# Where the rounded gate and value blocks are stored from: SyncE's queue or ScalarE's

## The chip, the cores and the metric

The kernel runs on one core of a Trainium2 chip. The metric is the device time of one execution in microseconds. Three runs of the kernel before took 806.23, 806.28 and 807.58 us; the median is 806.28 us. The core's engines are named as in the profile: PE (matrix products; PEld is its weight load), DVE (VectorE), ACT (ScalarE), POOL (GpSimd) and SP (SyncE, which here only issues DMAs). ACT can issue DMAs as well, between its own instructions.

## The reference

Attention with a learned position bias is followed by a gated feed-forward layer. The weights of the second part arrive as float64.

```
scores = (q @ k.T) / 8 + bias(w1, b1, w2)            # 4 batches, 8 heads, 576 positions, 64 dims
attn   = softmax(scores) @ v                          # laid out as x: 2304 tokens x 512
gate   = 1 / (1 + exp(-(x @ w_gate)))                 # w_gate: 512 x 1536
val    = x @ w_val                                    # w_val:  512 x 1536
out    = (gate * val) @ w_out                         # w_out:  1536 x 512
```

## The kernel before

The program has three stages: the bias tables, the attention, and the feed-forward layer (class `Moe`), of which the first weights are prepared while the attention still runs. The layer cuts the 2304 tokens into six chunks of 384 (`T`), and the 1536 hidden columns into twelve blocks f = 0 to 11. For each f there are three weight blocks (f, z): z = 0 gate, z = 1 value, z = 2 output. Products are formed from a high and a low part of each factor, three matmuls for one.

The first two chunks go by plain products. `run` walks a fixed list `ORDER` of 24 units (chunk, f). In a unit PE forms `pg` and `pu` (`gates`, L888; one PSUM buffer each), then the products `po` of the unit before (`outs`, L912). ACT takes the sigmoid of `pg` (L897), DVE multiplies it with `pu` (L898), ACT copies the high part `gh` (L899) and DVE subtracts for the low part `gl` (L900). The next unit's `pg` can only begin when the sigmoid has read the last one. The other four chunks are done later by products of sums of weight blocks, which read the rounded blocks back from a buffer in HBM, `scratch` (L964).

Between the matmuls the weight blocks are prepared, one call of `convert` at a time, in the program's own order (`manual_schedule`: each engine runs its instructions in the order of the code). A block arrives by `stage` (L829, 512 KB, float64 as pairs of int32). `begin` gives it a buffer `wm` (a pool of five) and these steps, of which each call of `convert` does those that are due:

- step 0: ACT takes the size of the upper word (L198), the first write to `wm`
- step 1: DVE clamps it (L201); step 2: DVE rounds in three instructions (L204, L207, L210)
- step 3, `upper`: ACT copies the high part (L849)
- step 4, `lower`: DVE subtracts for the low part (L854), and `keep` stores the rounded block: gate and value blocks of f = 3 to 11, 18 in all, go to `scratch` (L860, 256 KB); output blocks go with both parts to `parts` (L858)

The blocks of f < 3 (`pre`) were rounded and stored in the bias stage and take no part in this. A sixth block needs a `wm` buffer that an earlier block has left, by its last reader and by its store.

Two rules of the framework matter for what waits. First, each DMA that SP or ACT issues is given one of eight completion semaphores, `DMAHW0` to `DMAHW7`, in turn in the order of the code, whichever engine issues it; before it is issued, its engine waits until the last DMA on that semaphore has landed. In the lists below `[waits DMAHW7_49]` at a DMA is this wait. Second, `wm` buffers are handed out when the program is built, and the instruction that first writes one waits for the last users of it.

Of the kernel before, what the change touches and what calls it, by code (L numbers as in the profile page):

```python
# [186 lines left out]
def narrow(nc, t, lo, hi, eng, sized=None):  # L187

    f = t.bitcast(F32)

    def size():
        if sized:
            sized.tensor_scalar(out=t, in0=hi, scalar1=0x7FFFFFFF, scalar2=None, op0=ALU.bitwise_and)
        else:
            nc.scalar.activation(out=f, in_=hi.bitcast(F32), func=AF.Abs)  # L198

    def clamp():  # L200
        eng.tensor_scalar(out=f, in0=f, scalar1=float(2.0 ** -15), scalar2=float(122880 - 2.0 ** -7), op0=ALU.max, op1=ALU.min)  # L201

    def low():
        nc.vector.tensor_scalar(out=t, in0=t, scalar1=3, scalar2=0x3FFFFFFF, op0=ALU.logical_shift_left, op1=ALU.bitwise_and)  # L204

    def top():
        nc.vector.scalar_tensor_tensor(out=t, in0=hi, scalar=-0x40000000, in1=t, op0=ALU.bitwise_and, op1=ALU.bitwise_or)  # L207

    def tail():
        nc.vector.scalar_tensor_tensor(out=t, in0=lo, scalar=29, in1=t, op0=ALU.logical_shift_right, op1=ALU.bitwise_or)  # L210

    return size, clamp, low, top, tail
# [498 lines left out]
class Moe:  # L711
# [121 lines left out]
    def begin(self):  # L833

        nc, n = self.nc, self.begun
        self.begun += 1
        f, z = b = self.blocks[n]
        w = self.raw.pop(0)
        if b in self.pre:
            m, steps = w, []  # L840
        else:
            t = self.pools["wm"].tile([128, 4, 128], I32, name="wm")
            m, steps = t.bitcast(F32), list(zip((0, 1, 2, 2, 2), narrow(nc, t, w[:, :, :, 0], w[:, :, :, 1], CLENG(nc, f, z))))

        def upper():
            p = self.pools["wfirst" if n < 3 or (z == 2 and n > 5) else "wa"]
            t = p.tile([128, 2, 4, 128], F32R, tag="w", name=f"w{z}_{f}")
            self.wts[b] = t[:, 0], t[:, 1], t
            nc.scalar.activation(out=t[:, 0], in_=m, func=AF.Copy)  # L849

        def lower():
            hi, lo, _ = self.wts[b]
            self.full.add(b)
            LOENG(nc, f, z).tensor_tensor(out=lo, in0=m, in1=hi.bitcast(F32), op=ALU.subtract)  # L854

        def keep():
            if z == 2:
                nc.sync.dma_start(out=self.parts[f], in_=self.wts[b][2].bitcast(F32))  # L858
            elif b not in self.pre:
                nc.sync.dma_start(out=self.scratch[b], in_=m)  # L860

        self.going[n] = steps + [(3, upper), (4, lower), (4 if z < 2 else 12 if f < 2 else 6, keep)]

    def convert(self):

# [321 lines left out]
```

## Time and profile before

| | |
|---|---|
| median of three runs | 806.28 us |
| profiled execution | 806.44 us, of which the span of instructions is 804.7 us |
| PE busy | 774.0 us, 96% of the span |
| DVE, ACT, POOL busy | 664.5, 490.5 and 341.8 us |
| plain products of the feed-forward layer | from about 367 to 502 us of the span |

The page of the profile gives busy time by engine. In the tables by stretch each engine has its busy time and, in brackets, its number of instructions; then come PE's granted clock as a share of full speed, the mean share of the DMA engines and GB/s. In the rows in order of time the first number is the start in us from the span's start, the second the duration, then engine, line and tiles; brackets give how long the engine had stood idle before, and what ended that. `SPq` and `ACTq` are DMAs as the engine issues them: the row shows the issue alone, not the transfer. In the list of waits: total us, times, longest us.

### The profile page before, as it was taken

The numbers are of one execution on the slowest core, as the hardware profiler recorded it, in microseconds if no ns is written. First come the engines' busy times: TensorE is split into PE (matmuls) and PEld (weight loads), VectorE is DVE, ScalarE is ACT, GpSimd is POOL, SyncE is SP. The second block draws the span as 40 slices with busy tenths as digits, with TensorE's granted clock in tenths as the row PEclk, the third lists the DMA queues.
The fourth block names the chain that finished last, engine by engine and source line by source line (L and its number), as shares of the span: only waits on it lengthen the run. The fifth ranks groups of instructions, "written<-read, shape, count | busy, mean of one in ns | idle before, by whom it ended". The sixth has DMA issues, their size and how long they took to land.

```text
span 804.7 us, 17534 instructions
## 1 busy us (share of the span) xinstructions
PE 774.0 (96%) x6356; PEld 722.6 (90%) x6356; DVE 664.5 (83%) x1397; ACT 490.5 (61%) x1046; POOL 341.8 (42%) x400
## 2 busy tenths in 40 slices
PE   7999989999999999889999999999999999999997
PEld 4888879999999998889889999898899999999996
DVE  6788888999999998996799898979878977776663
ACT  6888769989989987873444434543444435433432
POOL 1332659899999988950000000315232330423100
PEclk9999999999999999999999999999999999999999
DMA  5534435655655667739999643646334305421202
GB/s 197 172 126 144 121 88 149 172 146 155 174 152 152 177 183 206 205 113 277 354 303 276 174 145 131 202 138 218 107 112 140 105 27 193 148 62 70 79 1 79
DMA packets 66694, 124.22 MB, mean 154 GB/s; under 512 B 7344, under 2 KB 28976, under 8 KB 66608
## 3 DMA queue, kind: packets, MB, share of 16 engines
q1 hardware_dynamic: 64688, 120.15, 49.3%
q10 hardware_dynamic: 1920, 2.95, 1.2%
q8 instruction: 50, 0.82, 0.4%
q14 instruction: 36, 0.29, 0.1%
HBM read 86.04 MB, written 27.60 MB: 141 GB/s over the span
## 4 chain that ended last, share of the span: by engine, by line
PE 73%; DVE 14%; ACT 5%; issue 3%; DMA 3%; POOL 0%; SPq 0%; ACTq 0%; DVEq 0%
PE po L912 16%; PE pu L1010 10%; PE pg L1010 10%; PE sc L560 8%; PE acc L645 8%; PE pt L583 6%; PE pg L888 5%; PE pu L888 5%; PE bps L353 3%; DVE btmp L361 2%; ACT ind L334 2%; PE y L329 2%; PE pt L603 1%; DVE en L564 1%; DVE bias L369 1%
## 5 line engine op out<-in xcount | busy, mean ns | idle before, releaser
L971 POOL TENSOR_TENSOR ws<-wm 128x256 f32<-128x256 f32 x44 | 38.5, 875 | 309.5 <-DVE g L898 148.2
L567 ACT ACTIVATE en<-en,mn 128x576 f32<-128x576 f32 x144 | 111.6, 775 | 31.0 <-DVE mn L564 29.9
L560 PE MATMUL sc<-k,QS 128*128 128x288 f32 x640 | 112.1, 301 | 1.4 <-DVE bias L369 0.6
L1010 PE MATMUL pu<-xq,wv 128*128 128x384 f32 x504 | 102.7, 339 | 1.7 <-DVE g L898 0.6
L1010 PE MATMUL pg<-xq,wv 128*128 128x384 f32 x504 | 102.8, 339 | 0.4 <-DVE u L1015 0.4
L564 DVE CUSTOM_DVE_ANT_0 en<-sc,bias 128x576 f32<-128x576 f32 x128 | 93.8, 752 | 7.1 <-PE sc L560 6.1
L1010 PEld LDWEIGHTS pg<-xq,wv 128*128 128x128 f32 x504 | 90.2, 188 | 8.5 <-DVE u L1015 1.7
L1010 PEld LDWEIGHTS pu<-xq,wv 128*128 128x128 f32 x504 | 89.8, 188 | 8.5 <-DVE c L1015 1.2
L560 PEld LDWEIGHTS sc<-k,QS 128*128 128x128 f32 x640 | 92.3, 189 | 2.5 <-PE sc L560 0.8
L583 PE MATMUL pt<-ident,en 128*128 128x128 f32 x576 | 87.5, 274 | 3.5 <-DVE aL L483 1.9
L912 PE MATMUL po<-wo,gh 128*128 128x512 f32 x288 | 89.6, 392 | 0.0
L645 PE MATMUL acc<-aH,vv 128*128 128x288 f32 x240 | 76.2, 334 | 2.7 <-DVE xe L648 2.7
L583 PEld LDWEIGHTS pt<-ident,en 128*128 128x128 f32 x576 | 68.9, 141 | 6.7 <-ACT en L567 2.9
L483 DVE TENSOR_TENSOR aL<-pt,aH 128x512 fp32r<-128x512 f32 (+1 forms) x112 | 66.6, 607 | 7.1 <-ACT aH L482 7.1
L353 PE MATMUL bps<-cfs,ind 128*128 128x64 bf16 x1458 | 67.4, 193 | 2.9 <-DVE bias L369 2.4
L334 ACT ACTIVATE ind<-y 128x576 bf16<-128x576 f32 x100 | 62.1, 654 | 10.2 <-PE y L329 7.9
L645 PE MATMUL acc<-aL,vv 128*128 128x288 f32 x240 | 67.1, 296 | 0.0
L353 PEld LDWEIGHTS <-ind 128*128 128x128 bf16 x1458 | 58.6, 98 | 9.2 <-DVE bias L369 4.2
L487 POOL TENSOR_TENSOR aL<-ar,aH 128x512 fp32r<-128x512 f32 x48 | 62.4, 1301 | 4.0
L482 ACT ACTIVATE aH<-pt 128x512 fp32r<-128x512 f32 (+1 forms) x112 | 57.4, 527 | 1.1 <-PE pt L583 1.1
L912 PE MATMUL po<-wo,gl 128*128 128x512 f32 x144 | 56.7, 394 | 0.0
L888 PE MATMUL pg<-xhi,w 128*128 128x384 f32 x192 | 53.4, 337 | 1.8 <-ACT g L897 1.8
(158 smaller groups left out, 1860.0 us busy)
## 6 DMA issues: line engine op xcount, KB each, us to landing
wm<-scratch SPq DMA_DIRECT2D x48, 256.0 KB, 2.7
wo<-parts SPq DMA_DIRECT2D x24, 512.0 KB, 5.1
kr<-in_k_dram SPq DMA_DIRECT2D x32, 288.0 KB
QS<-part SPq DMA_DIRECT2D x64, 144.0 KB, 2.7
xs<-xe SPq DMA_DIRECT2D x32, 288.0 KB, 3.4
xin<-xs SPq DMA_DIRECT2D x48, 192.0 KB, 4.4
parts<-w SPq DMA_DIRECT2D x12, 512.0 KB, 2.7
vr<-in_v_dram SPq DMA_DIRECT2D x16, 320.0 KB, 3.9
```

The costliest lines, as they stand in the source:

```text
L334: nc.scalar.activation(out=o, in_=y[:, :, 0:HF], func=AF.Sigmoid, scale=float(2.0 ** 64))
L353: nc.tensor.matmul(out=o, lhsT=st, rhs=cfs[:, part], start=(part == 0), stop=(part == 2))
L483: return lambda: nc.vector.tensor_tensor(out=lo, in0=ps, in1=hi.bitcast(F32), op=ALU.subtract)
L487: nc.gpsimd.tensor_tensor(out=lo, in0=src, in1=hi.bitcast(F32), op=ALU.subtract)
L560: nc.tensor.matmul(out=ps[:, e, 0:HF], lhsT=l, rhs=r[:, HF * e:HF * e + HF], start=(i == 0), stop=(i == len(mms) - 1))
L564: nc.vector.tensor_tensor_reduce(out=half(en), in0=ps[:, :, 0:HF], in1=half(nbias), scale=-0.125, scalar=3.0e38, op0=ALU.add, op1=ALU.min, ...
L567: nc.scalar.activation(out=en, in_=en, func=AF.Exp, bias=mn, scale=-1.0, accum_out=sm)
L583: nc.tensor.transpose(pt[:, J], en[:, 128 * J:128 * J + 128], ident)
L645: nc.tensor.matmul(out=acc[:, 0:HF], lhsT=l, rhs=r, start=(i == 0), stop=(i == len(mms) - 1))
L888: self.nc.tensor.matmul(out=(pg, pu)[z], lhsT=l, rhs=r, start=(kc == 0 and i == 0), stop=(kc == 3 and i == 2))
L912: self.nc.tensor.matmul(out=po, lhsT=l[:, tt], rhs=r, start=(first and i == 0), stop=(last and i == 2))
L1010: nc.tensor.matmul(out=p, lhsT=W[i][:, l, at + kc], rhs=V[b][:, r, kc], start=(n == 0), stop=(n == 5))
```

## The change

The store `keep` of the 18 gate and value blocks is issued by ACT instead of SP, and stands directly behind `upper`, in the call of `convert` before that of `lower`. Output blocks and the blocks of f < 3 keep their steps.

```
             elif b not in self.pre:
-                nc.sync.dma_start(out=self.scratch[b], in_=m)
-
-        self.going[n] = steps + [(3, upper), (4, lower), (4 if z < 2 else 12 if f < 2 else 6, keep)]
+                nc.scalar.dma_start(out=self.scratch[b], in_=m)
+
+        self.going[n] = steps + [(3, upper), *([(3, keep), (4, lower)] if z < 2 and b not in self.pre else [(4, lower), (4 if z < 2 else 12 if f < 2 else 6, keep)])]
```

PE, DVE and POOL have the same instructions in the same order. On ACT, from the first such block on (block (3,0), `w0_3`; the numbers behind names count tiles), before:

```order
L849 ACTIVATE w0_3_7626<-wm_7561 128x512 [waits DVE_49]
L198 ACTIVATE wm_7625<-ww_7452 128x512 [waits DMAHW5_49]
L897 ACTIVATE g_7677<-pg_7642 128x384 [waits PE_49,Activation_49]
L899 ACTIVATE gh_7678<-g_7677 128x384 [waits DVE_49]
L849 ACTIVATE w1_3_7686<-wm_7605 128x512
L198 ACTIVATE wm_7683<-ww_7497 128x512 [waits DMAHW0_49]
L849 ACTIVATE w2_3_7698<-wm_7617 128x512 [waits DVE_49]
L198 ACTIVATE wm_7695<-ww_7512 128x512 [waits DMAHW4_49,DMAHW1_49,Activation_49]
```

and now:

```order
L849 ACTIVATE w0_3_7626<-wm_7561 128x512 [waits DVE_49]
L860 DMA scratch_59<-wm_7561 128x512 [waits DMAHW7_49]
L198 ACTIVATE wm_7625<-ww_7452 128x512 [waits DMAHW5_49]
L897 ACTIVATE g_7678<-pg_7643 128x384 [waits PE_49,Activation_49]
L899 ACTIVATE gh_7679<-g_7678 128x384 [waits DVE_49]
L849 ACTIVATE w1_3_7686<-wm_7605 128x512
L860 DMA scratch_59<-wm_7605 128x512 [waits DMAHW0_49]
L198 ACTIVATE wm_7684<-ww_7497 128x512
L849 ACTIVATE w2_3_7698<-wm_7617 128x512 [waits DVE_49]
L198 ACTIVATE wm_7696<-ww_7512 128x512 [waits DMAHW1_49,DVE_49]
```

The store stands between the copy of the high part and the next block's size, ahead of the sigmoid, and waits on semaphore 7. The size of block (4,2), the last row of each list, had the buffer of block (3,0) and waited for its store (semaphore 4); now it has the buffer of block (3,2) and waits for DVE, for the low part of that block.

On SP, from the load of value block (6,1) on, before:

```order
L829 DMA ww_7633<-in_moe_w_val_dram 128x4x256 [waits DMAHW7_49]
L798 DMA xin_7636<-xs_57 64x2x384 [waits DMAHW0_49]
L798 DMA xin_7636<-xs_57 64x2x384 [waits DMAHW1_49]
L807 DMA xrec_7639<-rs_58 64x384 [waits DMAHW2_49]
L807 DMA xrec_7639<-rs_58 64x384 [waits DMAHW3_49]
L860 DMA scratch_59<-wm_7561 128x512 [waits DMAHW4_49,DVE_49]
L829 DMA ww_7693<-in_moe_w_out_dram 128x1024 [waits DMAHW5_49]
L860 DMA scratch_59<-wm_7605 128x512 [waits DMAHW6_49,DVE_49]
L829 DMA ww_7705<-in_moe_w_gate_dram 128x4x256 [waits DMAHW7_49]
```

and now:

```order
L829 DMA ww_7634<-in_moe_w_val_dram 128x4x256 [waits DMAHW7_49]
L798 DMA xin_7637<-xs_57 64x2x384 [waits DMAHW0_49]
L798 DMA xin_7637<-xs_57 64x2x384 [waits DMAHW1_49]
L807 DMA xrec_7640<-rs_58 64x384 [waits DMAHW2_49]
L807 DMA xrec_7640<-rs_58 64x384 [waits DMAHW3_49]
L829 DMA ww_7694<-in_moe_w_out_dram 128x1024 [waits DMAHW4_49]
L829 DMA ww_7705<-in_moe_w_gate_dram 128x4x256 [waits DMAHW5_49]
L829 DMA ww_7753<-in_moe_w_val_dram 128x4x256 [waits DMAHW6_49]
L858 DMA parts_60<-w2_3_7698 128x1024 [waits DMAHW1_49,DVE_49]
```

The two stores have left the list, and three loads close up. Semaphore 7, which the load of value block (6,1) holds in both, was next used by a load of SP (gate block (7,0)); now its next user is the store of block (3,0) on ACT.

## Rows read from the trace of the kernel before

**Rows 1.** The page, busy time by engine.

```profile
PE 774.0 (96%) x6356; PEld 722.6 (90%) x6356; DVE 664.5 (83%) x1397; ACT 490.5 (61%) x1046; POOL 341.8 (42%) x400
```

**Rows 2.** By stretch: busy us by engine (instructions), granted clock, DMA share, GB/s.

```profile
382.00:392.00 10.00, 10.00 (x56) 9.59 (x55) 6.00 (x12) 3.92 (x7) 0.00 (x0) 1.00 1.06 389
392.00:402.00 10.00, 8.45 (x42) 7.09 (x40) 9.00 (x17) 4.34 (x8) 0.00 (x0) 1.00 1.08 319
402.00:412.00 10.00, 8.19 (x43) 7.46 (x44) 9.62 (x19) 5.41 (x11) 0.00 (x0) 1.00 1.07 311
412.00:500.00 88.00, 88.00 (x469) 82.82 (x468) 78.75 (x153) 37.23 (x73) 0.00 (x0) 1.00 0.65 201
```

**Rows 3.** Chain that ended last, 385 to 412: start, us, what.

```profile
394.02 6.99 DMA scratch<-wm
```

**Rows 4.** ACT in order of time, 388 to 402.

```profile
388.20 0.64 ACT L849 ACTIVATE w<-wm 128x512 fp32r<-128x512 f32 x1 [0.69 <-DVE wm L210]
...
389.95 0.49 ACT L897 ACTIVATE g<-pg 128x384 f32<-128x384 f32 x1 [0.57 <-PE pg L888]
...
399.21 0.69 ACT L198 ACTIVATE wm<-ww 128x512 f32<-128x512 f32 x1 [3.56 <-DMA scratch<-wm]
...
401.11 0.66 ACT L198 ACTIVATE wm<-ww 128x512 f32<-128x512 f32 x1 [0.69 <-DMA scratch<-wm]
401.68 0.47 ACT L897 ACTIVATE g<-pg 128x384 f32<-128x384 f32 x1
```

**Rows 5.** DVE in order of time, 392 to 409.

```profile
392.04 0.56 DVE L898 TENSOR_TENSOR g<-pu,g 128x384 f32<-128x384 f32 x1 [0.82 <-PE pu L888]
...
398.43 0.68 DVE L854 TENSOR_TENSOR w<-wm,w 128x512 fp32r<-128x512 f32 x1
...
402.18 0.56 DVE L898 TENSOR_TENSOR g<-pu,g 128x384 f32<-128x384 f32 x1 [0.94 <-ACT g L897]
...
408.10 0.55 DVE L900 TENSOR_TENSOR gl<-g,gh 128x384 fp32r<-128x384 f32 x1
```

**Rows 6.** PE in order of time, 393 to 409.

```profile
393.83 0.34 PE L888 MATMUL pg<-xhi,w 128*128 128x384 f32 x1
...
402.20 0.44 PE L888 MATMUL pg<-xhi,w 128*128 128x384 f32 x1 [1.76 <-ACT g L897]
...
408.71 0.50 PE L912 MATMUL po<-w,gl 128*128 128x512 f32 x1 [1.61 <-DVE gl L900]
```

**Rows 7.** SP's DMA issues in order of time, 386 to 397.

```profile
386.11 0.68 SPq L829 DMA_DIRECT2D ww<-in_moe_w_val_dram  x1
...
390.63 0.34 SPq L860 DMA_DIRECT2D scratch<-wm  x1
...
396.56 0.38 SPq L829 DMA_DIRECT2D ww<-in_moe_w_gate_dram  x1
```

**Rows 8.** What SP's queue waited for, 394.3 to 396.6: total, times, longest.

```profile
SPq L829 <- DMA ww<-in_moe_w_val_dram: 2.2, 1, 2.2
```

**Rows 9.** ACT and its own DMA issues, 364 to 373.

```profile
364.26 0.63 ACT L849 ACTIVATE w<-ww 128x512 fp32r<-128x512 f32 x1 [1.67 <-DMA ww<-scratch]
364.29 0.33 ACTq L826 DMA_DIRECT2D ww<-scratch  x1
...
371.71 0.38 ACTq L829 DMA_DIRECT2D ww<-in_moe_w_out_dram  x1
372.14 0.63 ACT L849 ACTIVATE w<-ww 128x512 fp32r<-128x512 f32 x1 [1.11 <-DMA xs<-xe]
```

**Rows 10.** SP's issue of the reciprocals in a later cycle.

```profile
426.90 1.19 SPq L807 DMA_DIRECT2D xrec<-rs  x2
```

**Rows 11.** ACT in that cycle, the copy ahead of store (7,1).

```profile
436.48 0.64 ACT L849 ACTIVATE w<-wm 128x512 fp32r<-128x512 f32 x1 [0.77 <-DVE wm L210]
```

**Rows 12.** By stretch, in the attention, columns as in rows 2.

```profile
312.00:315.40 3.40, 1.73 (x11) 1.35 (x12) 3.37 (x6) 2.30 (x6) 3.32 (x4) 1.00 0.48 152
315.40:318.80 3.40, 3.40 (x16) 3.40 (x17) 2.67 (x7) 2.08 (x5) 3.32 (x4) 0.50 0.58 170
```

## The prediction

> **What bounds the kernel now.** I read the page first: PE is busy for 774.0 of 804.7 us [rows 1], so nearly every microsecond that another engine loses costs nothing unless PE stands still for it, and what has to be found is where PE stands still near these stores. The table by stretch answers that. PE is busy without a gap from 382 to 392 and from 412 to 500, but it loses 1.55 us in 392 to 402 and 1.81 us in 402 to 412 [rows 2]. That is the start of the 18 stores; in the long stretch with most of them PE never waits. In the two stretches with losses DVE is busy for 9.00 and 9.62 of 10 us: beside PE it is the second engine that is nearly full there.
>
> The chain of waits puts 6.99 us of just this place on the transfer of a store [rows 3]. ACT in order of time shows where it bites: the size of a new block stands 3.56 us and then 0.69 us until a store has left its buffer [rows 4]. Behind them in ACT's order is the sigmoid at 401.68, for which PE waited 1.76 us, and DVE 0.94 us [rows 4 to 6]. PE's second loss, 1.61 us at 408.71, is for `gl`, which comes so late because DVE has a queue of work in front of it: from 402.18 to 408.10 it has no gap [rows 5, 6].
>
> So the most that an earlier store can bring is small. DVE works without a gap from 392.04 until 401.24 (402.18 less its idle 0.94) [rows 5]; were ACT never held, DVE's multiplication at 402.18 could come 0.94 us sooner, `gl` too, and PE's restart at 408.71 too. The 1.76 us that PE wins ahead of it is given back in front of `gl`. The ceiling of the gain is 0.94 us, not 3.37.
>
> **The change part by part: the wait that it moves.** The store of block (3,0) is now in ACT's stream and waits for semaphore 7, that is for the load of value block (6,1). In the kernel before SP stood at that same wait: the load was issued at 386.11, and the next user of semaphore 7, a load of SP, went out at 396.56 after 2.2 us of waiting for it [rows 7, 8]. So the load lands at 396.5, 10.4 us after its issue. In the changed program everything ahead of this load is the same, and what was taken from SP's list stood behind it. I therefore take 396.56 for the moment at which ACT may issue the store. The row before has this store at 390.63 [rows 7]: the step is called one sooner, and it is issued 5.9 us later.
>
> What is queued behind it on ACT: the size of block (4,0), then the sigmoid that was at 389.95 [rows 4]. That ACT does not let an instruction pass a DMA is shown by its three loads at the layer's start: the copy at 372.14 begins 0.05 us after the last issue ends (371.71 plus 0.38), with 1.11 us of idle before it [rows 9]. These rows show a held-up issue, though no long semaphore wait on ACT. The Trainium skill, "Perfetto Trace Analysis", section "DMA Instruction — HWDGE (DVE, Sync)", says that the semaphore wait of such a DMA is spent on the issuing sequencer, ahead of the profiled start, and that the sequencer takes up its next instruction only after the issue. By that rule the whole wait is ACT's; without it the first rival below would be the forecast.
>
> Now the times, step by step. Issue at 396.56 for 0.33 us and 0.05 us to the next instruction [rows 9] gives the size at 396.94; the sigmoid follows 0.57 us after a size (401.11 to 401.68) and lasts 0.47 us [rows 4], so it ends at 397.98. DVE's multiplication starts 0.03 us behind (402.15 to 402.18): 398.01 instead of 392.04, which is 5.97 us late [rows 4, 5]. PE's `pg` starts 0.05 us behind: 398.03 instead of 393.83, so PE stands still for 4.2 us [rows 6].
>
> From there DVE has 9.20 us of work without a gap (392.04 to 401.24) and is through at 407.21. The next multiplication also needs the next sigmoid. Ahead of that on ACT is now a new wait: the size of block (4,2) waits for the low part of block (3,2), DVE's instruction at 398.43 that ends 7.07 us behind the multiplication (399.11 less 392.04) [rows 5], hence at 405.08. Behind it come a size, a copy and a size at 0.57 us each and a sigmoid of 0.47 us, 2.18 us: 407.3. So the multiplication that was at 402.18 is at 407.33, 5.15 us late. The lateness has shrunk by the 0.94 us of idle that goes, and grown by 0.12 us of waiting for ACT. After it DVE again has no gap up to `gl` at 408.10, now 413.25, and PE's restart moves from 408.71 to 413.86. From 412 on PE had no idle time to give back [rows 2], and everything that later engines and queues do is released by PE, DVE or ACT; the 5.15 us stay.
>
> **The smaller terms.** The other 17 stores add an issue each. One costs 0.33 us, and the row shows it running beside an activation that began 0.03 us earlier [rows 9]; from 412 to 500 ACT is busy for 37.23 of 88 us [rows 2]. I take nothing. With the cover gone it would be 18 times 0.33, 6.0 us. On SP 18 issues go; nothing there is late from 412 on, so nothing is won, and nothing can be lost by loads going out sooner. The waits for `wm` buffers (3.56 and 0.69 us) go: the store of (3,0) now has from 396.9 until the size of (5,0) at 406.2, 9.3 us, where it took at most 8.6 us before (390.63 to 399.21) [rows 4, 7]. If it took the 10.4 us of the load twice its size, 1.1 us would be added, and that is the upper bound; the lower is nothing.
>
> The later stores wait for semaphores too. The closest is that of a value block, whose semaphore a load of reciprocals had before it: that goes out from 426.90 on, the copy ahead of the store is at 436.48, 9.6 us later [rows 10, 11]. Even a landing as slow as 10.4 us would hold ACT for 0.8 us, which is the 0.77 us that it stood idle before this copy. I take nothing here; one such hold for each of the seven later pairs (f = 5 to 11) that reached PE is the far end: 5.6 us.
>
> The landing at 396.56 I take as good to 1 us, since a different mix of transfers follows it; lateness moves with it one to one, so the sum is 4.1 to 6.2 us.
>
> **Sum.** The profiled execution took 806.44 us, its span 804.7, and stands 0.16 us above the median. Plus 5.15: 811.6 on its own base, 811.4 against the median of 806.28, which I predict.
>
> **Rivals.**
>
> *ACT is not held.* If the issue waits somewhere else than in ACT's stream, or the load lands by 391, ACT keeps its times, the store is out at 388.9 (388.20 plus 0.64) [rows 4], and both buffer waits go. Then DVE's 0.94 us is all there is to win: 805.3 us. For it: the store no longer stands behind SP's waits. Against: the 10.4 us of the load, and rows 9. The point from which it decides is ACT's release: lateness is 5.15 us at 396.56, so none at 391.4, and a gain only before that.
>
> *PE loses its clock as well.* In the attention PE was busy for 1.73 of 3.40 us at the full grant, and the next 3.40 us were granted 0.50, that is 1.2 of 2.4 GHz [rows 12]. In the forecast PE stands still for 4.2 us and then again in front of `gl`. A halved grant right after 398 falls into time in which PE waits for DVE and costs little; one that falls behind 413.86, where PE sets the pace, costs half of 3.4 us, 1.7 us: 813.1, and with two of them 814.8. The Trainium skill, "TensorE: Matmul & The Clock Gate", section "HAM oscillation — how this bites in real kernels", describes the same: a wait for a DMA puts the array back to its low clock and the work behind starts there. Against it: 1.76 and 1.61 us of idle time here left the grant at 1.00 [rows 2, 6].
>
> *The stores hold ACT for every pair.* If issues or holds do not hide, 5.6 to 6.0 us come on top: about 817 us. Against it stands ACT's idle time in rows 2.
>
> *The hold is shorter.* The load lands between 392 and 395.5: 807 to 810.3 us. For it only that fewer stores share the DMA engines.
>
> **How the numbers follow.** Forecast, 4.1 to 6.2 us late: 0.68. Clock: 0.12. Holds for every pair: 0.04. Shorter hold: 0.06, plus 0.03 for a hold that comes out even. ACT not held: 0.07. From 808.5 to 814.5 us the range holds the forecast, nearly all of the clock's case and half of the shorter hold; I count that as 0.8, since each of these cases can also be missed in its size. The likeliest case alone is 810.4 to 812.5. A change of less than 0.2% (1.6 us) cannot be told from none here; faster by more than that is beyond even the first rival's 0.94 us, so 0.02; within it are the first rival and the even case with a few near them, 0.10; slower 0.88.
>
> **What would show it.** ACT idle for about 8 us between the copy of `w0_3` and the store's issue, ended by the load of a value block; PE idle for about 4.2 us at 393.8; no ACT wait for a store's transfer at the sizes; a new ACT wait of about 3.5 us for DVE's low part before the size of (4,2); DVE's `gl` near 413.2, and PE without a gap from about 414 on. The prediction is wrong if ACT takes the sigmoid near 390 as before, or if PE has new gaps behind 414.

## The result, and the profile after

The changed kernel took 812.39 us (median of four runs, 810.62 to 813.53), the kernel before 806.49 us beside it (four runs): a ratio of 1.0069, 95% interval 1.0051 to 1.0087. It is slower, by 5.9 us, where 5.15 us were predicted. The profiled execution took 812.0 us, its span is 810.2 us. One execution of e2 (1952 us) and one of before beside e5 to e8 (2688 us) lie far above all others and are left out of the medians and ratios below.

ACT in order of time, after; these rows answer to [rows 4].

```profile
389.50 0.63 ACT L849 ACTIVATE w<-wm 128x512 fp32r<-128x512 f32 x1 [0.69 <-DVE wm L210]
397.19 0.35 ACTq L860 DMA_DIRECT2D scratch<-wm  x1
397.58 0.66 ACT L198 ACTIVATE wm<-ww 128x512 f32<-128x512 f32 x1 [7.45 <-DMA ww<-in_moe_w_val_dram]
398.15 0.48 ACT L897 ACTIVATE g<-pg 128x384 f32<-128x384 f32 x1
399.24 0.52 ACT L899 ACTIVATE gh<-g 128x384 fp32r<-128x384 f32 x1 [0.62 <-DVE g L898]
399.25 0.33 ACTq L860 DMA_DIRECT2D scratch<-wm  x1
...
405.77 0.68 ACT L198 ACTIVATE wm<-ww 128x512 f32<-128x512 f32 x1 [3.51 <-DVE w L854]
405.78 0.34 ACTq L860 DMA_DIRECT2D scratch<-wm  x1
...
407.43 0.48 ACT L897 ACTIVATE g<-pg 128x384 f32<-128x384 f32 x1
```

The first row is the copy of the high part of block (3,0). Then ACT stands still for 7.45 us, and what ends it is the load of a *value block*, not the store: the row of the store itself has 0.35 us. By the order of the program the load on semaphore 7 is that of (6,1), which SP issues at 389.50 in this run:

```profile
389.50 0.67 SPq L829 DMA_DIRECT2D ww<-in_moe_w_val_dram  x1
```

The size and the sigmoid of the unit stand behind it. The second store (399.25) runs beside the copy of `gh` and costs nothing, and the old waits for `scratch<-wm` at the sizes are gone. In their place stands the new wait of 3.51 us for DVE's low part.

DVE and PE after, beside [rows 5, 6]:

```profile
398.65 0.56 DVE L898 TENSOR_TENSOR g<-pu,g 128x384 f32<-128x384 f32 x1 [6.13 <-ACT g L897]
...
407.94 0.56 DVE L898 TENSOR_TENSOR g<-pu,g 128x384 f32<-128x384 f32 x1
```

```profile
398.68 0.55 PE L888 MATMUL pg<-xhi,w 128*128 128x384 f32 x1 [3.87 <-ACT g L897]
399.86 1.01 PE L888 MATMUL pg<-xhi,w 128*128 128x384 f32 x2 [0.32 <-DVE w L854]
407.96 0.45 PE L888 MATMUL pg<-xhi,w 128*128 128x384 f32 x1 [0.87 <-ACT g L897]
414.47 0.50 PE L912 MATMUL po<-w,gl 128*128 128x512 f32 x1 [1.61 <-DVE gl L900]
```

DVE's idle time before the second multiplication, 0.94 us before, is gone: from 398.65 on its rows show no wait, and all that follows is as late as the sigmoid made it. PE restarts behind `gl` at 414.47 instead of 408.71. By stretch (columns as in [rows 2]):

```profile
392.00:402.00 10.00, 5.82 (x23) 4.59 (x22) 3.80 (x9) 3.03 (x6) 0.00 (x0) 0.84 1.08 331
402.00:416.00 14.00, 11.52 (x59) 10.08 (x58) 13.61 (x27) 6.67 (x13) 0.00 (x0) 0.99 0.83 261
416.00:504.00 88.00, 88.00 (x469) 82.78 (x468) 78.75 (x151) 37.98 (x73) 0.00 (x0) 1.00 0.67 205
398.86:402.27 3.41, 3.09 (x9) 2.58 (x9) 3.34 (x7) 2.25 (x4) 0.00 (x0) 0.50 1.05 365
402.27:405.60 3.33, 3.33 (x20) 3.16 (x20) 3.26 (x7) 0.00 (x0) 0.00 (x0) 1.00 0.46 168
```

From 416 on PE has no gap, with 13 of the 18 stores in that time: nothing is lost there, and nothing is won back. The fourth row shows the granted clock at half for 3.41 us right behind PE's stand of 3.87 us; what it cost is told below.

### The profile page after: what moved, and what is told of

It is laid out like the page before. It is cut to its first block, busy times and chain, and to the rows that moved or that the text cites. A ratio compares the mean times of both kernels' runs of the same rounds, so it can differ in the third digit from the quotient of the medians.

```text
span 810.2 us, 17521 instructions
## 1 busy us (share of the span) xinstructions
PE 775.9 (96%) x6356; PEld 723.0 (89%) x6356; DVE 665.7 (82%) x1397; ACT 490.9 (61%) x1046; POOL 341.2 (42%) x400
## 4 chain that ended last, share of the span: by engine, by line
PE 70%; DVE 15%; ACT 5%; DMA 4%; issue 4%; POOL 1%; SPq 1%; ACTq 0%; DVEq 0%
PE po L912 15%; PE pu L1010 10%; PE pg L1010 10%; PE sc L560 8%; PE acc L645 8%; PE pt L583 6%; PE pu L888 4%; PE pg L888 4%; DMA ww<-in_moe_w_val_dram 3%; PE bps L353 3%; DVE btmp L361 2%; PE y L329 2%; PE pt L603 1%; DVE bias L369 1%; ACT ind L334 1%
```

## The experiments

Theory 1 is the prediction's: a store on ACT's queue waits for the last user of its completion semaphore, and ACT stands meanwhile. Theory 2: a store holds ACT by itself, for its issue or its transfer. Theory 3: many small costs, of 18 issues or of two queues in each other's way. Each experiment ran beside the kernel before on its chip, in five rounds (5 to 12 runs of each kernel, 22 to 35 of before). Before took 806.67 us (median) beside e1 to e4 and beside e9 to e11, and 807.66 us beside e5 to e8; the ratios are estimated from all runs of both kernels and so can differ a little from the ratio of two medians.

**e1: only the store of (3,0) moves.**

```
-                nc.sync.dma_start(out=self.scratch[b], in_=m)
+                (nc.scalar if b == (3, 0) else nc.sync).dma_start(out=self.scratch[b], in_=m)
...
-        self.going[n] = steps + [(3, upper), (4, lower), (4 if z < 2 else 12 if f < 2 else 6, keep)]
+        self.going[n] = steps + [(3, upper), *([(3, keep), (4, lower)] if b == (3, 0) else [(4, lower), (4 if z < 2 else 12 if f < 2 else 6, keep)])]
```

> Only the store of block (3,0) is on ScalarE's queue, at the earlier step; the other 17 stay on SyncE at the old step. In this program's order the store has semaphore 5, whose user before it is the load of an output block, issued at 384.85 in the trace of before and landed near 391.9, not semaphore 7 with the value block (6,1), landed near 396.6. Theory 1 (ACT is held until the user of the semaphore ahead has landed): ACT held at this store until about 392, 0.5 us of lateness left, 806.8 us (806.0 to 808.0). Theory 2 (a store holds ACT for its own transfer or issue, whatever its semaphore): held for the same 7.5 us as in the change, 811 to 812 us. Theory 3 (the loss is the sum of many stores or of two queues in each other's way): one eighteenth, 806.8 us as well, and no long hold in ACT's rows.

Measured: 806.95 us, ratio 1.0007 (0.9995 to 1.0018). ACT in order of time:

```profile
388.81 0.64 ACT L849 ACTIVATE w<-wm 128x512 fp32r<-128x512 f32 x1 [0.59 <-DVE wm L210]
393.10 0.35 ACTq L860 DMA_DIRECT2D scratch<-wm  x1
393.49 0.66 ACT L198 ACTIVATE wm<-ww 128x512 f32<-128x512 f32 x1 [4.05 <-DMA ww<-in_moe_w_out_dram]
```

The same store from the same place holds ACT for 4.05 us instead of 7.45, and what ends it is the load of the output block that holds semaphore 5. So the hold is set by whose semaphore the store gets; theory 2 falls.

**e2: all but the first pair move.** The reverse of e1, for both blocks of f = 3.

```
-                nc.sync.dma_start(out=self.scratch[b], in_=m)
+                (nc.sync if f == 3 else nc.scalar).dma_start(out=self.scratch[b], in_=m)
```

The earlier step is for f > 3 alone, in the same way.

> The stores of blocks (3,0) and (3,1) stay on SyncE at the old step; the 16 others are as in the change. Theory 1: none of the 16 meets an unlanded user of its semaphore while PE waits for ACT, so the time is that of before, 806.5 us (805.6 to 807.5), with the two old waits for store transfers (3.6 and 0.7 us) back at the sizes. Theory 3: 16/18 of the loss, 811 to 812 us. Theory 2: held at the store of (4,0) instead, 811 to 812 us.

Measured: 805.92 us, ratio 0.9985 (0.9973 to 0.9998). Sixteen of the 18 moved stores cost nothing; theory 3 falls. The old waits for store transfers are back at the sizes, as expected (2.82 and 0.68 us in its trace). With e1 and e2 the loss sits in the first pair, and in its wait; of the two stores, the rows of the change show only the first held. The kernel is even 1.2 us faster than before by this ratio, and PE's wait for the sigmoid behind the sizes is 1.0 us instead of 1.76:

```profile
PE pg L888 <- ACT g L897: 1.0, 1, 1.0
```

**e3: no store moved, three DMAs of 64 bytes on ACT's queue.**

```
             nc.scalar.activation(out=t[:, 0], in_=m, func=AF.Copy)
+            for i in range(3 * (b == (3, 0))):
+                nc.scalar.dma_start(out=self.spare[i:i + 1, 0, 0:16], in_=m[i:i + 1, 0, 0:16])
```

> The kernel before with all its stores on SyncE, and three added DMAs of 64 bytes each on ScalarE's queue behind the rounding of block (3,0), to a spare place in DRAM. In the order they take semaphores 5, 7 and 0, whose users before them are the load of an output block, the value block (6,1) and an input part. Theory 1: ACT is held at them until the last of these has landed, near 397 on the scale of before: 812 us (810.5 to 814), though 192 bytes are moved. Theory 2 and theory 3: three issues of 0.33 us, 806.5 to 807.5 us.

Measured: 812.15 us, ratio 1.0063 (1.0050 to 1.0077): the whole loss, with 192 bytes. ACT in order of time:

```profile
389.89 0.63 ACT L850 ACTIVATE w<-wm 128x512 fp32r<-128x512 f32 x1 [0.69 <-DVE wm L210]
393.64 4.40 ACTq L852 DMA_DIRECT2D scratch<-wm  x3
398.09 0.66 ACT L198 ACTIVATE wm<-ww 128x512 f32<-128x512 f32 x1 [7.57 <-DMA xin<-xs]
```

The three issues are grouped into one row, from the start of the first to the end of the third; that they take 4.40 us together, and that the hold ends with the landing of an input part, fits issues that go out one by one as the loads on their semaphores land. This kernel also moves the semaphores of SP's next loads by three, so it is not free of side effects, but the length of the hold and its price are those of the change. The mean granted clock of its profiled execution is 0.945, against 0.990 to 0.992 in its four other runs; PE's busy time is still that of the change (776.7 and 775.9 us) and the time is the median of the five, so the result does not hang on it.

**e4: the whole change, with four loads ahead of the store issued by GpSimd,** so that the store gets another semaphore.

```
-            t[n, "in"], t[n, "rec"] = self.load_x(c, k), self.load_r(c, k)
+            one = nc.gpsimd if (c, k) == (2, 0) else None
+            t[n, "in"], t[n, "rec"] = self.load_x(c, k, one), self.load_r(c, k, one)
```

> The whole change, and besides the four loads of input and reciprocals that stand between the value block (6,1) and the store in the order (for one 384-column part) are issued by GpSimd, which has semaphores of its own. So the store of (3,0) gets semaphore 3, whose user before it landed before 389. Theory 1: ACT is not held, 805.4 us (804.8 to 806.8), lower than before by the 0.94 us that DVE stood idle, if GpSimd's four issues disturb nothing. Theory 2 and theory 3: 811 to 812 us, as the change.

Measured: 807.43 us, ratio 1.0012 (0.9998 to 1.0025). Most of the loss is gone with all 18 stores still on ACT's queue, but the 805.4 us expected of it were missed: the user of semaphore 3 had not landed. GpSimd and SP in order of time:

```profile
370.60 1.41 POOL L798 DMA_DIRECT2D xin<-xs  x2 [7.56 <-DVE xlo L817]
372.00 1.05 POOL L807 DMA_DIRECT2D xrec<-rs  x2
```

```profile
385.43 0.38 SPq L829 DMA_DIRECT2D ww<-in_moe_w_gate_dram  x1
389.44 0.38 SPq L829 DMA_DIRECT2D ww<-in_moe_w_val_dram  x1
```

GpSimd had nothing ahead of these loads and put them out at 370.60, where SP did so at 386.83 before; the order of the other loads' semaphores moved with them, and SP's value block (5,1) went out at 389.44 instead of 382.71. It landed at 395.19 and held ACT for 2.05 us:

```profile
395.58 0.66 ACT L198 ACTIVATE wm<-ww 128x512 f32<-128x512 f32 x1 [2.05 <-DMA ww<-in_moe_w_val_dram]
```

The hold was where the theory put it, on the load that the order names; the error was to think that load in time. (1.8 us of the 6.7 us stood already at 369 in this run; that the four loads put off the rest is argued from the order, and no run shows it by itself. The profiled execution took 809.78 us, 2.4 us above the median, so most executions may have had less of all this.)

**e5: the step alone.** `nc.sync` as before, the earlier step for all 18.

> All 18 stores one step sooner as in the change, but on SyncE's queue as before. In this order the store of (3,0) has semaphore 7 with an old user that has long landed, and SyncE stands until DVE has merged the block. Theory 1 (the loss is ACT held at the first store for a load on its semaphore): ACT has no hold, since it issues no store; 806.3 us (805.3 to 807.5). Rival (the earlier step itself makes it late, since loads go out behind the stores or the buffers are handed round differently): 810 us or more.

Measured: 807.53 us, ratio 1.0000 (0.9986 to 1.0013). The step costs nothing and brings nothing.

**e6: the queue alone.** `nc.scalar` for all 18, the steps as before.

> All 18 stores on ScalarE's queue as in the change, but at the old step, behind the low part. The store of (3,0) keeps semaphore 7 and so the load of value block (6,1), but it now stands in ACT's order behind the size of (4,0), the sigmoid and the copy of gh. Theory 1: ACT held for about 4 us instead of 7.5 (from 393.1 to 397.2 on the scale of before), the sigmoid at 389.95 is not late, DVE meets it at the low part of (3,1) at 395.24, about 3.0 us late less the 0.94 us of idle: 808.5 us (807.3 to 810). Rival (any store on ACT's queue costs the same, wherever it stands): 812 us. Rival (only the earlier step costs): 806.5 us.

Measured: 809.91 us, ratio 1.0027 (1.0015 to 1.0039), that is 2.2 us above its own before, where 2.0 us were expected (808.5 less 806.5). ACT in order of time:

```profile
391.77 0.49 ACT L897 ACTIVATE g<-pg 128x384 f32<-128x384 f32 x1 [0.56 <-PE pg L888]
394.46 0.52 ACT L899 ACTIVATE gh<-g 128x384 fp32r<-128x384 f32 x1 [2.19 <-DVE g L898]
398.40 0.34 ACTq L860 DMA_DIRECT2D scratch<-wm  x1
398.79 0.63 ACT L849 ACTIVATE w<-wm 128x512 fp32r<-128x512 f32 x1 [3.81 <-DMA ww<-in_moe_w_val_dram]
...
413.50 0.66 ACT L198 ACTIVATE wm<-ww 128x512 f32<-128x512 f32 x1 [4.32 <-DMA scratch<-wm]
```

It is the same semaphore and the same load, but the store stands behind the sigmoid here, so ACT is held for 3.81 us, and less of what PE waits for is behind it. The last row is a wait that I had not foreseen, a size that stands 4.32 us for the transfer of a store; behind it PE lost 0.62 us. So the near hit has a second, small part.

**e7: all 18 on GpSimd's queue, at the earlier step.** `nc.gpsimd` for `nc.scalar`.

> All 18 stores at the earlier step, issued by GpSimd, which has nothing to compute here and semaphores of its own that no load uses. Theory 1: no hold on ACT, and no wait of the sizes for a store behind SyncE's queue: 805.4 us (804.8 to 807), at most 0.94 us better than before, since DVE has no more idle time there. The loads are then out sooner, and DMA engines were full from 382 to 412 in all kernels so far, so a later landing may eat the gain: 806.5 us. Rival (the loss comes from the store going out sooner and colliding with loads): 809 us or more.

Measured: 806.41 us, ratio 0.9989 (0.9979 to 1.0000). In its trace ACT has neither the hold nor a size that waits for a store's transfer, and GpSimd's issues take 0.54 to 0.74 us each. The sooner stores that collide with loads (809 us) are out. The gain is at the edge of what this comparison tells.

**e8: the first pair on GpSimd's queue, the others on ACT's.**

```
-                nc.scalar.dma_start(out=self.scratch[b], in_=m)
+                (nc.gpsimd if f == 3 else nc.scalar).dma_start(out=self.scratch[b], in_=m)
```

> The change, but the stores of (3,0) and (3,1) are issued by GpSimd; the 16 others on ScalarE's queue, all at the earlier step. Theory 1: the whole loss goes, and the time is that of the kernel before or up to 0.94 us better: 805.6 us (804.8 to 807). Rival (a store of a later pair takes up the hold, since semaphores shift by two): ACT held at the store of (4,0) for a load on its semaphore, 808 to 812 us.

Measured: 805.52 us, ratio 0.9983 (0.9969 to 0.9996). Taking the first pair away from ACT takes the whole loss away, with the other 16 stores where the change has them, and no later store took up the hold. It does what e2 did, without the waits for stores behind SP's queue.

**e9 to e11: the change, e8 once more, and e8 with the other 16 stores left on SP.**

> The changed kernel once more, as the yardstick beside the next two. Theory 1: 1.007 times the time of before (1.005 to 1.009), with ACT held behind the rounding of (3,0) by the load of a value block.

> The kernel with the stores of (3,0) and (3,1) issued by GpSimd and the other 16 by ScalarE, again. Theory 1: 0.998 to 0.9995 times the time of before (0.3 to 1.6 us less), by the 0.94 us of DVE's idle time that goes. Rival (its earlier lead came from the spread of before alone): 1.000 within 0.001.

> Only the stores of (3,0) and (3,1) leave SyncE, for GpSimd, one step sooner; the 16 others stay on SyncE at the old step. Theory 1: all that an earlier store can bring lies at the first pair, so the time is that of the kernel with the others on ScalarE: 805.6 us on a chip where before takes 806.5 (0.998 to 1.000). Rival (the later stores bring something on ScalarE's queue): that of before, 1.000, or above.

Measured: the change 811.71 us, 1.0059 (1.0044 to 1.0074); e8 again 805.19 us, 0.9982 (0.9970 to 0.9995); e11 805.98 us, 0.9992 (0.9979 to 1.0005). So the version with the first pair on GpSimd beats both kernels: before by about 1.4 us, twice, and the change by 6.5 us (811.71 less 805.19). Its rows in e10, for PE's waits from 380 to 420 (total, times, longest):

```profile
PE po L912 <- DVE gl L900: 1.6, 1, 1.6
PE pg L888 <- ACT g L897: 0.9, 1, 0.9
```

Before, the second of these was 1.76 us [rows 6]: PE's loss is 0.86 us smaller. That this gain comes from moving the first pair is not shown, though: e2 leaves that pair on SP, and its wait (1.0 us) and its ratio (0.9985) are nearly the same. Whether the 16 others gain something on ACT's queue stays open too: the intervals of e2, e10 and e11 overlap.

## Why the prediction was right

**The wait and whose it is.** Shown. ACT stood still between the copy of `w0_3` and the store, ended by the load of (6,1), 7.45 us where about 8 were forecast, and e3 made a hold of the same length out of three DMAs of 64 bytes, while e1 shortened it with another semaphore. The rule taken from the Trainium skill ("Perfetto Trace Analysis", section "DMA Instruction — HWDGE (DVE, Sync)"), that such a wait is spent on the issuing sequencer ahead of the profiled start, agrees with the rows: 0.35 us in the row of the issue, 7.45 us of idle around it.

**The chain behind it.** The prediction says that, with ACT's size at 396.94, PE restarts behind `gl` at 413.86, and that lateness moves one to one with the release. Five traces, of four kernels, have a hold ahead of the sigmoid of this unit, at five different moments:

| kernel | size after the hold | restart by the chain: 413.86 + size − 396.94 | PE's restart in the trace |
|---|---|---|---|
| change | 397.58 | 414.50 | 414.47 |
| e9, change again | 396.42 | 413.34 | 413.30 |
| e4 | 395.58 | 412.50 | 412.46 |
| e3 | 398.09 | 415.01 | 414.81 |
| e1 | 393.49 | 410.41 | 410.21 |

All agree to 0.2 us. This carries the two terms on which the sum rests: the 0.94 us of DVE's idle time that cushions the delay, and the 0.12 us of new wait for DVE's low part (9.29 us between the two multiplications after, 9.32 forecast). ACT has no such wait in e1 and e3; there 9.12 and 9.13 us lie between the multiplications, which is most of their 0.2 us. The cushion is a number of one trace: in e2 and e5, where SP stores the first pair as before, DVE is idle there for 0.2 and 0.7 us.

**The size.** The sum gave 5.15 us, the profiled executions differ by 5.56, PE's restarts by 5.76, the medians by 5.9. Not all of that is the change's. The last products ahead of PE's stand, which the change does not touch, start 0.82 us later in this profile than before, and 0.34 us earlier in e9. These are their starts (before, change, e9), and the store's issue and PE's restart in e9:

```profile
391.77 0.62 PE L912 MATMUL po<-w,gh 128*128 128x512 f32 x2
392.59 0.62 PE L912 MATMUL po<-w,gh 128*128 128x512 f32 x2
391.43 0.62 PE L912 MATMUL po<-w,gh 128*128 128x512 f32 x2
396.03 0.35 ACTq L860 DMA_DIRECT2D scratch<-wm  x1
413.30 0.50 PE L912 MATMUL po<-w,gl 128*128 128x512 f32 x1 [1.62 <-DVE gl L900]
```

| us behind the start of these products | before | change | e9 |
|---|---|---|---|
| the next user of semaphore 7 is issued | 4.79 | 4.60 | 4.60 |
| PE's restart | 16.94 | 21.88 | 21.87 |

Counted so, the delay is 4.94 and 4.93 us, 0.2 us under the sum. The landing, which the prediction took from the trace of before and held good to 1 us, came 0.19 us sooner. The sum itself carries 0.04 us too much, since 2.18 us behind 405.08 is 407.26 and not 407.3. The stand of 4.2 us was counted from the start of `pg`; from the end of the last product (394.00 before), as the rows count it, it would be 4.03, against 3.87 in the trace. What the profiled execution has beyond 4.94 us was there before the store, or came behind the restart, and that it brings the difference near to 5.15 again is chance. By the medians the change cost 5.9 us in the first comparison and 5.0 us in the second (811.71 less 806.67); 4.9 and 5.15 lie within both intervals.

**The clock.** This rival came true in its mechanism and not in its price. Behind PE's stand of 3.87 us the granted clock was 0.50, that is 1.2 of 2.4 GHz, for 3.41 us. PE needed more time for that work, and then waited the less for DVE: its later waits of 0.87 and 1.61 us were both still there, so DVE set the restart, as the chain has it to 0.03 us. It fell into the time that the prediction names as the cheap one.

**The smaller terms.** Eighteen issues at nothing: shown by e2 (16 of them) and by the rows where an issue runs beside an activation. Holds at later pairs: none, by e2 and by the 88 us without a gap. No wait for `wm` buffers after the hold: as forecast. The ceiling of the gain, 0.94 us: with the hold taken away, e10's PE waits 0.86 us less than before (e2's 0.8 us less), and by their ratios e8 and e10 are 1.4 and 1.5 us faster, with intervals of 0.3 to 2.5 us that hold 0.94; whether there is more to win than 0.94 they do not tell.

## What to carry to other kernels

Ahead of moving a DMA to an engine that computes, look up which transfer last used its completion semaphore and when that landed: in these runs ACT stood until then, and everything behind it in its order too, however small the moved DMA was. On an engine with nothing to compute here, and with semaphores that no load had, the stores cost nothing (e7, e8); behind the sigmoid that PE waits for, the same wait cost 2.2 us instead of 5 to 6 (e6). And a delay on the path is passed on less the idle time that the next engine had. To compare two traces, count from the last instruction that the change cannot touch: the program can be late before it.

## What was not expected of the hardware

The same 512 KB load took 10.4 us before, 7.7 us in the profile of the change and 9.1 us in e9 (386.95 to 396.03), with the DMA engines' share at 1.02 to 1.08 from 392 to 402 in all three. It looks as if the landing varied, but against the program's own progress it is the issue that does. Behind the start of the products shown under the size, semaphore 7 was free after 4.79, 4.60 and 4.60 us, and after 4.80 us in e6 (398.40 less 393.60), while SP issued the load 5.66, 3.09, 4.48 and 4.45 us ahead of that start (before, change, e9, e6). An issue up to 2.6 us earlier brought no earlier landing. What fixes the landing no run shows.
